# Attention, a wide first layer and a soft expert layer on one core: reordering the seam between two batches

## The chip, the cores and the metric

The kernel runs on one core of a Trainium2 chip. A core has five engines with instruction queues of their own: TensorE (PE, matrix products into PSUM), VectorE (DVE), ScalarE (ACT), GpSimd (POOL) and SyncE (SP), which here only issues the loads and stores (DMAs). Each engine takes its instructions in the order in which the program lists them and waits for other engines by semaphores. The metric is the device time of one execution in microseconds, lower is better. Before the change it is 446.04 us, the median of three runs (444.56 to 446.34).

## The reference

Three layers follow one another; all inputs are fp32 except the first layer's weights, which arrive as 64-bit floats.

1. Attention over 4 batches, 8 heads, 576 positions, 64 dimensions per head. A query sees keys in a causal window of 32 positions (heads 0 to 3), or every fourth key in a window of 128 (heads 4 to 7). `scores = q k^T / 8`, softmax over the window, times `v`.
2. `h = x @ w_in` (2304 x 512 times 512 x 2048), `g = h - tanh(h)`, `g @ w_out` (2048 x 512).
3. `logits = x @ phi` (32 slots). A softmax over all tokens gives the slots' inputs, 8 experts with two matrices and a relu work on 4 slots each, and a softmax over the slots mixes the results back for each token.

The kernel never forms the second layer's output for all tokens: it folds `phi` into `w_out` (`wp = w_out @ phi`) and takes the logits straight from `g`.

## The kernel before, in words

Heads go in pairs. `PO = (2, 3, 0, 1)` is the order of the pairs, so "the first pair" of a batch is pair 2. A pair has three units of scores, so a batch has 12 units, numbered in that order.

Batch 0's attention comes first. Its work is laid out with a small planner: `at(t, f, args)` puts a function on a list with a due time, and the list is sorted and run, so a due time only sets the place in the program order, which is the order on every engine and on SP. On the same list stand the first six row blocks of `w_out`, the first four column blocks of `w_in`, and the first two blocks of the first layer's products (`emit_h`).

A block of 64-bit weights becomes fp32 in three steps. `conv_a` (ACT, L514) takes the upper words, `conv_b` shifts them and ors in the lower words (DVE, L522 and L523). For `w_in`, `conv_in_c` then rounds to a high part (L103, on DVE for blocks 0 and 1, on ACT for 2 and 3) and subtracts it from the value, which gives the low part (POOL, L536). The products need both: `emit_h` adds `w_hi x_hi + w_hi x_lo + w_lo x_hi` (L581 to L583) over four parts of the depth. For `w_out`, `conv_out_c` and `conv_out_d` transpose the block, multiply it with `phi` (L555, copied by DVE) and store the fp32 block to DRAM (L551).

From then on chunk 0 (batch 0's first 512 tokens) goes through the first layer in eight mixed steps `s = 0 .. 7`, two blocks a step, and batch 1's attention is done inside them: `mixed_step`. The order within a step is, in short: the step's weight loads (`load_w`), batch 1's loads (`an.load`), the first block's products, `turn_qk`, the norms of the last scores, tanh (ACT, L587) and subtraction (DVE, L590) of the block, the second block likewise, the transposes of the last probabilities (PE, L408), conversions, the scores of units 2s and 2s + 1 (mask product L344, scores L366, maxima on DVE L381, exponentials on ACT L384), `scale_q` for the pair that is turned next, and the logits (L599). `QKS = (0, 1, 2, 4)` are the steps in which the four pairs are turned.

Batch 1's q and k are loaded in blocks of 32 x 32 (`load_qk_blocks`, L245 and L247, eight DMAs of 72 KB a pair in runs of 128 bytes). `scale_q` multiplies q by 1/8 on ACT (L255). `turn_qk` transposes k (L267) and then q (L268) on DVE into one of two buffers. The scores read that buffer. Batch 1's first pair is loaded during batch 0's attention.

The raw 64-bit weights of the first steps lie in `gt`, the buffer for the transposed `g`, in four places (`RAW`), so a weight load waits until the block that lay there has been shifted. Step 1's load of `w_out` (block 8) takes the place of block 6, which step 0 converts; step 2's load of block 10 takes that of `w_in` block 4.

The lines that the change touches set these places: the time of `conv_a("in", 3)`, the time of `conv_in_c` for blocks 0 and 1, the time of `scale_q(1, PO[0])`, the `turn_qk` of the first pair, and the table of `an.load(nqk, nv)`: up to how many pairs of q and k, and of v, are loaded by that step. Before, the table has `0: (3, 2)`: step 0 loads the second pair's q, k and v and the third pair's q and k.

Of the kernel before, what the change touches and what calls it, by code (L numbers as in the profile page):

```python
# [32 lines left out]
PO = (2, 3, 0, 1)  # L33
# [31 lines left out]
def moe_kernel(ctx: ExitStack, tc: tile.TileContext, q, k, v, w_in, w_out, phi, w1, w2, out):  # L65
# [186 lines left out]
    def scale_q(b, p):  # L252
        t = raws[b, p]
        if b in EA:
            nc.scalar.activation(out=t[:, 0], in_=t[:, 0], func=ACTF.Copy, scale=0.125)  # L255
        else:
            nc.gpsimd.tensor_scalar(out=t[:, 0], in0=t[:, 0], scalar1=0.125, scalar2=None, op0=ALU.mult)

    def turn_qk(b, p):

        if not qks:
            t = sb.tile([128, 2, 2 * S], F32, tag="qk", name="qk")
            qks.append(Ring([t[:, 0], t[:, 1]]))
        t = raws[b, p]
        qT[b, p] = qks[0].next()
        kT[b, p] = qT[b, p][:, S:2 * S]
        nc.vector.transpose(out=kT[b, p], in_=t[:, 1])  # L267
        nc.vector.transpose(out=qT[b, p][:, 0:S], in_=t[:, 0])  # L268
# [202 lines left out]
    def emit_lows():  # L471
        while lows:
            lows.pop(0)()
# [4 lines left out]
    def load_w(kind, ft):  # L478

        if ft % 2:  # L480
            return
        place = RAW.get((kind, ft))
        if place is None:
            t = unit("raww", [128, 1024], I64)
        else:
            t = gt[:, 4 * place:4 * place + 4].rearrange("p a b -> p (a b)").bitcast(I64)
        if kind == "in":
            t = t.rearrange("p (k f) -> p k f", k=KT)
            nc.sync.dma_start(out=t, in_=w_in[:, 128 * ft:128 * ft + 256].rearrange("(k p) f -> p k f", p=128))
            w = t.bitcast(U32).rearrange("p k (i f two) -> p two i k f", i=2, two=2)  # L490
        else:
            t = t.rearrange("p (i d) -> p i d", i=2)
            nc.sync.dma_start(out=t, in_=w_out[128 * ft:128 * ft + 256, :].rearrange("(i p) d -> p i d", p=128))
            w = t.bitcast(U32).rearrange("p i (d two) -> p two i d", two=2)
        for i in range(2):
            raw_t[kind, ft + i] = w[:, 0, i], w[:, 1, i]
# [12 lines left out]
    def conv_a(kind, ft):  # L509

        f = convs[kind].next()
        hw = raw_t[kind, ft][1].bitcast(F32)

        nc.scalar.activation(out=like(f, kind), in_=hw, func=ACTF.Prelu, scale=2.0 ** -112, alpha=-2.0 ** 32)  # L514
        cvt[kind, ft] = f

    def conv_b(kind, ft):
        wl, _ = raw_t.pop((kind, ft))
        f = cvt[kind, ft]
        du = f.bitcast(U32)  # L520
        dk = like(f, kind).bitcast(U32)
        nc.vector.tensor_scalar(out=du, in0=du, scalar1=3, scalar2=None, op0=ALU.logical_shift_left)  # L522
        nc.vector.scalar_tensor_tensor(  # L523
            out=dk, in0=wl, scalar=29, in1=dk, op0=ALU.logical_shift_right, op1=ALU.bitwise_or
        )
# [14 lines left out]
    def conv_out_c(ft):  # L540
        f = cvt["out", ft]
        ps = mm([128, 4, 128])
        for dt in range(4):
            nc.tensor.transpose(ps[:, dt, :], f[:, 128 * dt:128 * dt + 128], ident)
        wt = convs["wt"].next()
        copy(ENGS["wt"][ft % 2], wt, ps)
        wstate["wt", ft] = wt

    def conv_out_d(ft):
        f = cvt.pop(("out", ft))  # L550
        nc.sync.dma_start(out=wo_dram[128 * ft:128 * ft + 128, :], in_=f)  # L551
        wt = wstate.pop(("wt", ft))
        part = mm([128, 128])
        for dt in range(4):
            nc.tensor.matmul(  # L555
                part[32 * dt:32 * dt + 32, :], lhsT=phi_sb[:, dt, :], rhs=wt[:, dt, :],
                start=True, stop=True, tile_position=(0, 32 * dt),
            )
        if ft % 4 == 0:
            wstate["wq"] = convs["wq"]  # L560
        copy(ENGS["wq"], wstate["wq"][:, ft % 4, :], part)

    def conv_out_e(ft):
        if ft % 4 == 3:
            wq = wstate.pop("wq")
            ps = mm([128, 4, 32])
            for i in range(4):
                nc.tensor.matmul(ps[:, i, :], lhsT=wq[:, i, :], rhs=stack[:, 0, :], start=True, stop=True)
            copy(ENGS["wp"], wp[:, ft - 3:ft + 1, :], ps)
# [4 lines left out]
    def emit_h(xh, xl, ft, ps=None, part=range(KT)):  # L574

        if ps is None:
            ps = ps_h.tile([128, 512], F32, tag="h", name="h")[:, 0:xh.shape[-1]]
        for n in part:
            kt = PO[n]
            wh, wl = win(0, ft)[:, kt, :], win(1, ft)[:, kt, :]  # L580
            nc.tensor.matmul(ps, lhsT=wh, rhs=xh[:, kt, :], start=(n == 0), stop=False)  # L581
            nc.tensor.matmul(ps, lhsT=wh, rhs=xl[:, kt, :], start=False, stop=False)  # L582
            nc.tensor.matmul(ps, lhsT=wl, rhs=xh[:, kt, :], start=False, stop=(n == KT - 1))  # L583
        return ps

    def emit_tanh(ps, g):
        nc.scalar.activation(out=g, in_=ps, func=ACTF.Tanh)  # L587

    def emit_sub(ps, g):
        nc.vector.tensor_tensor(out=g, in0=ps, in1=g, op=ALU.subtract)  # L590
# [13 lines left out]
    def emit_gT(ch, ft, g):  # L604

        nc.vector.transpose(out=gt[:, ft, :], in_=g)  # L606
# [279 lines left out]
    def emit_first(ch, xh, xl, ft, first):  # L886

        return emit_h(xh, xl, ft, first[ft], range(3, KT)) if ch == 0 and ft < 2 else emit_h(xh, xl, ft)

    with tc.manual_schedule():  # L890
# [4 lines left out]
        def at(t, f, *args):  # L895
            steps.append((t, len(steps), f, args))

        for b, (t0, dt) in enumerate((ATT0,)):
            for i in range(NU):
                t = t0 + dt * i  # L900
# [18 lines left out]
        for e in range(KA):  # L919
            t, dt = WO1[0] + WO1[1] * e, WO1[1]  # L920
# [6 lines left out]
        for e in range(4):  # L927
            t, dt = WI[0] + WI[1] * e, WI[1]
            at(t - LWI if e < 2 else 45.0, load_w, "in", e)
            at(t, conv_a, "in", e)  # L930
            at(t + 3.3, conv_b, "in", e)
            at(t + (5.4 if e < 2 else 3.4), conv_in_c, e)
        first = []
        for i in range(2):

            at(ATT0[0] + ATT0[1] * (12.6 + 0.4 * i), lambda i: first.append(emit_h(xhi[0], xlo[0], i, part=range(3))), i)
        at(56.0, scale_q, 1, PO[0])
        for _, _, f, args in sorted(steps, key=lambda s: s[0:2]):
            f(*args)
        emit_lows()  # L940
# [14 lines left out]
        def mixed_step(an, ch, s, xh, xl, gs, posts):  # L955

            a, b = 2 * s, 2 * s + 1
            if s < 5:
                load_w("out", 6 + a)
            if s < 6:  # L960
                load_w("in", 4 + a)
            an.load(*{0: (3, 2), 2: (4, 3), 3: (4, 4)}.get(s, (0, 0)))
            pa, gs[a] = emit_first(ch, xh, xl, a, first), gring.next()
            if s in QKS:
                turn_qk(an.b, PO[QKS.index(s)])
            an.norms(s - 1)
            if s:
                for n in (a - 2, a - 1):
                    emit_gT(ch, n, gs[n])
            emit_tanh(pa, gs[a])  # L970
            if 0 < s < 7:
                conv_a("in", 2 + a)
                conv_a("in", 2 + b)
            emit_sub(pa, gs[a])
            emit_lows()
            if 0 < s < 7:
                conv_b("in", 2 + a)
            pb, gs[b] = emit_first(ch, xh, xl, b, first), gring.next()
            emit_tanh(pb, gs[b])
            emit_sub(pb, gs[b])  # L980
            if 0 < s < 6:
                conv_out_c(4 + a)
                conv_out_c(5 + a)
            an.trans(s)
            if s in (2, 4, 6):
                conv_out_e(3 + a)
            if 0 < s < 6:
                conv_out_d(4 + a)
                conv_out_d(5 + a)
            if 0 < s < 7:  # L990
                conv_in_c(2 + a)
                conv_b("in", 2 + b)
                conv_in_c(2 + b)
            if s < 5:
                conv_a("out", 6 + a)
                conv_a("out", 7 + a)
            an.score(2 * s, 2 * s + 1)
            if s < 5:
                conv_b("out", 6 + a)
                conv_b("out", 7 + a)  # L1000
            an.values(s)
            if s + 1 in QKS:
                scale_q(an.b, PO[QKS.index(s + 1)])
            if s:
                emit_logits(ch, a - 1, gs[a - 1])
            emit_logits(ch, a, gs[a])
# [36 lines left out]
        QKS = (0, 1, 2, 4)  # L1043
        an = Attn(1)
        an.nqk, an.nv, posts = 1, 1, None
        for ch in range(4):
# [34 lines left out]
            an, posts = nxt, last_posts  # L1081
# [198 lines left out]
```

## Time and profile before

The profiled execution took 444.48 us, its span (first to last instruction) 442.7 us, so 1.8 us lie around the span.

| | busy, us | share of the span |
|---|---|---|
| PE products | 413.1 | 93% |
| PE weight loads | 303.4 | 69% |
| DVE | 254.1 | 57% |
| ACT | 204.7 | 46% |
| POOL | 77.2 | 17% |

Shares of the chain of work that ended last over the whole span: PE 60%, issue 13%, DVE 11%, ACT 9%, DMA 3%, SP's queue 2%.

How to read it. The chain is followed back from the last instruction: at each step to what released it, or to the instruction before it on its engine. Busy shares are means over stages: in the attention of batch 0 and in the mixed steps (to about 130 us) DVE is busy five to nine tenths of a slice and ACT two to eight tenths, in the later chunks both less and PE nine tenths. The granted clock of PE is 9 tenths or more in 38 of 40 slices of the span; it is lower in the slice from 55 to 66 us and in the last one. In a timeline, a row's first number is its start, the second its duration (several instructions of one kind are merged, "x2"), and the bracket at the end gives the engine's idle time before it and what ended it. For SP, a duration is the time that the issue took, not that of the transfer.

### The profile page before, as it was taken

What the parts mean: (1) busy time and instruction counts of PE and PEld (TensorE: products, weight loads), DVE (VectorE), ACT (ScalarE), POOL (GpSimd) and SP (SyncE); (2) the same over time, 40 slices, a digit from 0 to 9 for tenths busy, and PEclk for the clock granted to TensorE, in tenths of its full rate; (3) what the DMA queues carried; (4) which work ended last, traced back from release to release, by engine and by line L of the source; (5) the groups of instructions that cost most, each with busy time, mean ns of one, the idle gap of its engine ahead of it and who ended that gap; (6) DMA issues with size and microseconds to landing.
All of it is one profiled execution on the core that took longest, in us unless ns stands there. A gap on an engine that the chain in (4) does not pass through costs nothing.

```text
span 442.7 us, 11369 instructions
## 1 busy us (share of the span) xinstructions
PE 413.1 (93%) x4564; PEld 303.4 (69%) x4564; DVE 254.1 (57%) x611; ACT 204.7 (46%) x707; POOL 77.2 (17%) x95
## 2 busy tenths in 40 slices
PE   6989979998999999999999999999999999999980
PEld 4766658876777767877767777776777688556330
DVE  1576688989976767765767865636444332223050
ACT  3677668778862546563363655231121233223040
POOL 3131233232344312122030311000000000010000
PEclk9999989999999999999999999999999999999996
DMA  8989899799567032522405203292005599999938
GB/s 228 253 206 301 237 188 278 227 285 318 178 109 130 2 51 46 95 41 66 94 5 90 44 2 97 80 415 79 0 1 179 185 408 409 364 403 407 394 134 304
DMA packets 102022, 81.17 MB, mean 183 GB/s; under 512 B 78032, under 2 KB 81872, under 8 KB 101968
## 3 DMA queue, kind: packets, MB, share of 16 engines
q1 hardware_dynamic: 101968, 80.43, 60.7%
q8 instruction: 36, 0.59, 0.6%
q14 instruction: 18, 0.15, 0.1%
HBM read 71.50 MB, written 8.91 MB: 182 GB/s over the span
## 4 chain that ended last, share of the span: by engine, by line
PE 60%; issue 13%; DVE 11%; ACT 9%; DMA 3%; SPq 2%; POOL 1%; POOLq 0%; ACTq 0%
PE h L581 10%; PE h L583 9%; PE h L582 9%; ACT mem L384 5%; PE mm L366 3%; PE h L806 3%; PE y L833 3%; PE lg L599 3%; PE mm L721 3%; PE mm L408 3%; PE mm L429 3%; PE warm L209 2%; SPq L247 2%; DMA wo_dram<-cva 1%; DVE gt L606 1%
## 5 line engine op out<-in xcount | busy, mean ns | idle before, releaser
L581 PE MATMUL h<-xhi,wts 128*128 128x512 f32 x256 | 104.9, 410 | 0.0
L583 PE MATMUL h<-xhi,wts 128*128 128x512 f32 x256 | 100.6, 393 | 0.8 <-POOL wts L536 0.8
L582 PE MATMUL h<-xlo,wts 128*128 128x512 f32 x256 | 100.5, 393 | 0.0
L587 ACT ACTIVATE mem<-h 128x512 f32<-128x512 f32 x72 | 42.8, 596 | 111.1 <-PE h L583 103.7
L590 DVE TENSOR_TENSOR mem<-h,mem 128x512 f32<-128x512 f32 x72 | 48.7, 678 | 62.6 <-ACT mem L587 62.6
L399 POOL TENSOR_TENSOR mem<-mem 128x320 f32<-128x320 f32 (+1 forms) x48 | 33.0, 695 | 159.7 <-DVE mem L398 71.4
L581 PEld LDWEIGHTS h<-xhi,wts 128*128 128x128 f32 x256 | 48.6, 190 | 15.6 <-issue 5.7
L583 PEld LDWEIGHTS h<-xhi,wts 128*128 128x128 f32 x256 | 48.4, 189 | 12.4 <-POOL wts L536 1.6
L582 PEld LDWEIGHTS h<-xlo,wts 128*128 128x128 f32 x256 | 48.6, 190 | 8.9
L606 DVE STREAM_TRANSPOSE gt<-mem 128x512 f32<-128x512 f32 x64 | 41.0, 682 | 0.0
L384 ACT ACTIVATE mem<-mem 128x80 f32<-128x80 f32 (+1 forms) x84 | 29.7, 355 | 15.9 <-DVE mem L381 15.9
L384 ACT ACTIVATE mem<-mm,mem 128x80 f32<-128x80 f32 (+1 forms) x84 | 26.6, 328 | 12.8 <-DVE mem L396 7.9
L103 ACT COPY mem<-mm 80x448 f32<-80x448 f32 (+4 forms) x64 | 25.7, 435 | 6.1 <-PE mm L408 5.0
L408 PE MATMUL mm<-mem 112*80 112x112 f32 (+1 forms) x168 | 23.8, 271 | 3.1 <-POOL mem L399 1.8
L429 PE MATMUL mm<-mem,v 80*64 80x48 f32 (+1 forms) x672 | 26.0, 226 | 0.5 <-ACT mem L103 0.5
L599 PE MATMUL lg<-mem 128*32 128x128 f32 x576 | 24.7, 280 | 1.3 <-ACT mem L621 0.7
L429 PEld LDWEIGHTS mm<-mem,v 80*64 80x64 f32 (+1 forms) x672 | 22.1, 137 | 4.6 <-ACT mem L103 1.0
L366 PE MATMUL mm<-qk 64*64 64x96 f32 (+2 forms) x672 | 23.4, 246 | 1.8 <-DVE qk L268 1.8
L366 PEld LDWEIGHTS mm<-qk 64*64 64x64 f32 (+1 forms) x672 | 17.9, 132 | 8.3 <-issue 4.6
L408 PEld LDWEIGHTS mm<-mem 112*80 112x80 f32 (+1 forms) x168 | 16.0, 122 | 8.6 <-POOL mem L399 4.1
L599 PEld LDWEIGHTS lg<-mem 128*32 128x32 f32 x576 | 13.6, 109 | 12.1 <-issue 9.0
L465 DVE TENSOR_TENSOR xlo<-mm,xhi 128x144 fp32r<-128x144 f32 (+4 forms) x72 | 15.9, 265 | 7.0 <-ACT xhi L103 7.0
(188 smaller groups left out, 632.1 us busy)
## 6 DMA issues: line engine op xcount, KB each, us to landing
ex<-in_moe_w_dram SPq DMA_DIRECT2D x21, 1024.0 KB, 11.1
gt<-in_moe_w_out_dram SPq DMA_DIRECT2D x7, 1024.0 KB, 7.4
gt<-in_moe_w_in_dram SPq DMA_DIRECT2D x7, 1024.0 KB, 8.8
gt<-in_moe_w_dram SPq DMA_DIRECT2D x6, 1024.0 KB, 10.0
mem<-in_moe_w_dram SPq DMA_DIRECT2D x5, 1024.0 KB, 7.2
wo_dram<-cva SPq DMA_DIRECT2D x16, 256.0 KB, 6.1
wo<-wo_dram SPq DMA_DIRECT2D x4, 1024.0 KB, 7.3
out_dram<-o SPq DMA_DIRECT2D x8, 512.0 KB, 4.8
```

The lines of the kernel that those rows point to most:

```text
L366: nc.tensor.matmul(ps[64 * y:64 * y + nr, c, :], lhsT=qT[b, p][r, q0:q0 + step * (nr - 1) + 1:step], rhs=kT[b, p][r, k0:k0 + step * (nk - ...
L384: nc.scalar.activation(out=pr[:, c, :], in_=ps[:, c, :], func=ACTF.Exp, bias=nm[:, c:c + 1], accum_out=sm[:, c:c + 1],)
L399: nc.gpsimd.tensor_tensor(out=pr, in0=pr, in1=rc.unsqueeze(2).to_broadcast([128, nb, nk]), op=ALU.mult)
L408: nc.tensor.transpose(ps[:, c, :], pr[0:P, c, :], ident[0:P, 0:P])
L429: nc.tensor.matmul(o[64 * hh:64 * hh + 64, col:col + nq], lhsT=vt[b, p](n, hh), rhs=pt[:, c, 64 * (x ^ sw):64 * (x ^ sw) + nq], start=True ...
L581: nc.tensor.matmul(ps, lhsT=wh, rhs=xh[:, kt, :], start=(n == 0), stop=False)
L582: nc.tensor.matmul(ps, lhsT=wh, rhs=xl[:, kt, :], start=False, stop=False)
L583: nc.tensor.matmul(ps, lhsT=wl, rhs=xh[:, kt, :], start=False, stop=(n == KT - 1))
L587: nc.scalar.activation(out=g, in_=ps, func=ACTF.Tanh)
L590: nc.vector.tensor_tensor(out=g, in0=ps, in1=g, op=ALU.subtract)
L599: nc.tensor.matmul(lgs[ch][row:row + 32, 0:128], lhsT=wp[:, ft, :], rhs=g[:, 128 * j:128 * j + 128], start=(ft < step), stop=(ft >= NFT - ...
L606: nc.vector.transpose(out=gt[:, ft, :], in_=g)
```

## The change

On the planner's list, block 3's `conv_a` moves 0.65 earlier (before the conversion of block 2 is finished by `conv_in_c`), `conv_in_c` of block 1 moves ahead of `conv_out_d` of the `w_out` blocks 4 and 5 (block 0's keeps its place in the order), `scale_q` of batch 1's first pair moves from 56.0 to 53.0, ahead of the last `emit_pv` of batch 0, and `turn_qk` of that pair comes onto the list at 54.85, behind `conv_b` of block 2 and ahead of its `conv_in_c` and of `conv_b` of block 3. In the mixed steps, step 0 no longer turns a pair, and the third pair's q and k are loaded in step 1, behind that step's two weight loads, instead of in step 0.

```diff
         for e in range(4):
             t, dt = WI[0] + WI[1] * e, WI[1]
             at(t - LWI if e < 2 else 45.0, load_w, "in", e)
-            at(t, conv_a, "in", e)
+            at(t if e < 3 else t - 0.65, conv_a, "in", e)
             at(t + 3.3, conv_b, "in", e)
-            at(t + (5.4 if e < 2 else 3.4), conv_in_c, e)
+            at(t + (5.25 if e < 2 else 3.4), conv_in_c, e)
...
-        at(56.0, scale_q, 1, PO[0])
+        at(53.0, scale_q, 1, PO[0])
+        at(54.85, turn_qk, 1, PO[0])
...
-            an.load(*{0: (3, 2), 2: (4, 3), 3: (4, 4)}.get(s, (0, 0)))
+            an.load(*{0: (2, 2), 1: (3, 2), 2: (4, 3), 3: (4, 4)}.get(s, (0, 0)))
             pa, gs[a] = emit_first(ch, xh, xl, a, first), gring.next()
-            if s in QKS:
+            if s and s in QKS:
                 turn_qk(an.b, PO[QKS.index(s)])
```

## Rows read from the trace of the kernel before

**Rows 1.** Waits of PE, 44 to 130 us: us in total, times, longest.
```profile
PE mm L366 <- DVE qk L268: 1.8, 1, 1.8
PE h L583 <- POOL wts L536: 0.6, 1, 0.6
```

**Rows 2.** Timeline of the seam, 54 to 64 us, all engines.
```profile
55.19 0.29 DVE L103 COPY cvb<-mm 128x128 f32<-128x128 f32 x1 [1.72 <-PE mm L555]
...
55.89 0.28 ACT L103 CAST xhi<-mm 128x144 fp32r<-128x144 f32 x1 [2.93 <-PE mm L429]
55.89 1.28 POOL L536 TENSOR_TENSOR wts<-mem,wts 128x512 fp32r<-128x512 f32 x1 [4.07 <-DVE wts L103]
...
56.54 0.92 DVE L522 TENSOR_SCALAR cvb<-cvb 128x512 uint32<-128x512 uint32 x1
...
59.31 0.67 ACT L255 ACTIVATE rqk<-rqk 128x576 f32<-128x576 f32 x1
...
59.44 1.06 DVE L522 TENSOR_SCALAR mem<-mem 128x512 uint32<-128x512 uint32 x1 [1.26 <-ACT mem L514]
...
60.39 0.44 PE L344 MATMUL mm<-mem 64*128 64x320 bf16 x2
60.54 0.69 DVE L523 SCALAR_TENSOR_TENSOR mem<-gt,mem 128x512 uint32<-128x512 uint32 x1
61.15 0.77 DVE L267 STREAM_TRANSPOSE qk<-rqk 128x576 f32<-128x576 f32 x1
...
62.50 1.25 DVE L590 TENSOR_TENSOR mem<-h,mem 128x512 f32<-128x512 f32 x2
...
63.37 0.48 PE L599 MATMUL lg<-mem 128*32 128x128 f32 x8
```

**Rows 3.** Timeline, DVE, shifts of step 0 with POOL idle.
```profile
64.47 0.41 DVE L522 TENSOR_SCALAR cva<-cva 128x512 uint32<-128x512 uint32 x1
...
65.97 0.69 DVE L523 SCALAR_TENSOR_TENSOR cva<-gt,cva 128x512 uint32<-128x512 uint32 x1
```

**Rows 4.** Busy time by window: us, five engines, granted clock, DMA share, GB/s.
```profile
64.00:67.00 3.00, 3.00 (x8) 2.32 (x9) 2.93 (x7) 2.80 (x18) 0.00 (x0) 0.50 1.30 208
```

**Rows 5.** Timeline of SP: weight loads of steps 0, 1, 2 and 3.
```profile
49.50 0.88 SPq L489 DMA_DIRECT2D gt<-in_moe_w_in_dram  x1
...
68.38 0.43 SPq L493 DMA_DIRECT2D gt<-in_moe_w_out_dram  x1
...
74.72 0.38 SPq L493 DMA_DIRECT2D gt<-in_moe_w_out_dram  x1
79.20 0.38 SPq L489 DMA_DIRECT2D gt<-in_moe_w_in_dram  x1
...
91.51 0.49 SPq L493 DMA_DIRECT2D raww<-in_moe_w_out_dram  x1
```

**Rows 6.** Lines L247 (50 to 64 us), L245 (79 to 90): issue ns, first and last start.
```profile
L247 SPq DMA_DIRECT2D rqk<-in_k_dram x4: 496/740/1212, 58.6 to 61.4; - x4
...
L245 SPq DMA_DIRECT2D rqk<-in_k_dram x4: 496/502/1009, 86.2 to 88.3; - x4
```

**Rows 7.** DMA issues near 61.4, 88.3 and 91.5 us: KB, median us to landing.
```profile
rqk<-in_k_dram SPq DMA_DIRECT2D x2, 72.0 KB, 2.8
...
rqk<-in_k_dram SPq DMA_DIRECT2D x2, 72.0 KB, 2.7
...
raww<-in_moe_w_out_dram SPq DMA_DIRECT2D x1, 1024.0 KB, 7.5
```

**Rows 8.** Timeline, mixed step 2 and the end of step 3's conversions.
```profile
79.03 0.77 DVE L267 STREAM_TRANSPOSE qk<-rqk 128x576 f32<-128x576 f32 x1
...
80.45 0.78 DVE L268 STREAM_TRANSPOSE qk<-rqk 128x576 f32<-128x576 f32 x1 [0.65 <-ACT rqk L255]
...
83.11 0.35 PEld L408 LDWEIGHTS mm<-mem 112*80 112x80 f32 x4 [0.42 <-POOL mem L399]
...
100.33 1.22 ACT L514 ACTIVATE cva<-raww 128x512 f32<-128x512 f32 x2
```

## The prediction, before the result was known

> **What bounds the kernel now.** I read the table of busy times first: TensorE (PE) is busy 93% of the span, so in most stages only its own work counts. Then the granted clock over the span, which is whole except near the end and in one slice, around 55 to 66 us. That is the seam between batch 0's attention and the first h step, and it is where the change lies. The table of PE's waits between 44 and 130 us [rows 1] shows what PE lost there: 1.8 us on the turned q and k of batch 1's first pair, 0.6 us on the low words of the second first-layer block. The timeline of the seam [rows 2] shows why the turn is late: VectorE (DVE) does the shifts of blocks 2 and 3 first (L522, L523) and sits idle for block 3's words from ScalarE (ACT); ACT itself sits idle 2.93 us before 55.89 and scales q only at 59.31. The scaling and the two turns (from 61.15) wait for nothing but their place in the order.
>
> From the second mixed step to about 120 us the chain of work that ended last runs mostly through DVE and ACT, not PE. In step 2 the turn of q waits 0.65 us for ACT, and PE's transposes wait 0.42 us for the probabilities that come after it [rows 8]. So a delay on DVE or ACT there reaches PE, and after that PE is so full that nothing gives it back.
>
> **Part 1: block 1's low words sooner.** conv_in_c(1) moves ahead of two copies of conv_out_d on DVE, which wait for PE anyway: DVE idles 1.72 us before 55.19 [rows 2], so it is free from 53.5. Its cast and GpSimd's (POOL's) subtraction, 1.28 us [rows 2], are done by about 55.2, when PE is still in the products before block 1. PE's 0.6 us wait goes, and PE reaches the mask product of the scores at 59.8 instead of 60.4. On the other engines nothing is added.
>
> **Part 2: scaling and turning ahead.** scale_q, 0.67 us [rows 2], falls into ACT's idle 2.93 us: free. If ACT had no such hole it would cost its 0.67 us. The block 3 words move ahead of it and of block 2's cast, so DVE no longer idles for them. DVE then runs: block 2's shift at 56.54 as before, but POOL's subtraction is no longer beside it. With POOL beside it L522 took 0.92 us [rows 2], without it 0.41 us [rows 3]. So block 2 ends at 56.54 + 0.41 + 0.69 = 57.6. The two turns now take from 61.15 to 62.50, 1.35 us up to the next start [rows 2]; behind block 2 they end at 59.0. Block 3's L522 starts there instead of at 59.44. But now POOL's subtraction of block 2 lies beside it until about 59.7, so I let it last to 60.0, and L523 starts at 60.0 instead of 60.54: a gain of 0.5 us, not more (bounds: 0.4 with the old duration of 1.06 us, 1.1 if it runs unhindered).
>
> What is late next on PE: the scores can run from 60.2, when the turned q and k are there. Behind them on PE stand the logits (L599), which need DVE's first subtraction of the step (L590), which needs ACT's tanh, which stands behind ACT's cast of block 3, which needs L523. That chain has moved only 0.5 us: 62.50 becomes 62.0, and the logits at 63.37 become 62.9 [rows 2]. So of 1.8 + 0.6 us on PE about 0.5 us reaches the next step; the rest is idle time put behind the scores instead of ahead of them. DVE's last shift of the step, which ends at 65.97 + 0.69 = 66.66 [rows 3], ends at about 66.15.
>
> The clock: the granted clock is 0.50 from 64 to 67 [rows 4], the lower level of 1.2 GHz, after PE's thin stretch from 60.4 to 63.4. In the changed order the thin stretch is from 59.8 to 62.9, about as long, so I leave this cost in, moved. If it went, 3 us at half rate would give back 1.5 us on PE.
>
> **Part 3: the third pair's loads.** This is the part that can cost. The sync queue (SP) issues in order. Today the third pair's q and k, eight loads, go out in step 0, and step 1's two 1 MB weight loads follow from 68.38 [rows 5]. After the change the weights stand first. The first of them must wait for the shift that ends at 66.15 (its place in gt holds the words that are shifted), so the two go out at about 66.15 and 66.6, two microseconds sooner than now, and the eight small loads behind them. Then come step 1's two stores and step 2's loads.
>
> How long do q and k take behind such weights? The trace has two cases. In step 0 the second weight load went out at 49.50, with the first half a microsecond ahead, and the last k at 61.4, landing 2.8 us later, at 64.2: 14.7 us [rows 5 to 7]. In step 2 the weight load went out at 79.20, the other one 4.5 us ahead of it, and the last k at 88.3, landing at 91.0: 11.8 us [rows 5 to 7]. From 66.6 that is 78.4 to 81.3. The new place is like step 0's in its order, but with less in flight before it, so I take the middle, 79.85.
>
> When is k needed? L267 of step 2 starts at 79.03 now [rows 8]; with the gain of 0.5 it would be 78.5. L268 follows at 80.45 since it waits for ACT; that would be 79.95. With k at 79.85, L267 runs 0.77 us from then and L268 starts at about 80.65: 0.2 us later than before. The gain is gone. At the low end (78.4) it stays; at the high end L268 is at 82.1, 1.65 us late. Behind L267 on DVE queue the reciprocals that POOL's products and PE's transposes wait for, so this passes to PE in full.
>
> By the Trainium skill, "DMA: Bandwidth & Descriptors", section "Anatomy of one DMA", a transfer takes about 2.0 us and its bytes at 436 GB/s (stated for the software path). For these 2.7 MB an estimate by that page is 8.2 us, k landing near 74.3, well in time. The trace does not agree: a single weight load of 1 MB took 7.5 us to land [rows 7]. The same page's section "Queues, rings and completion order" says that each engine takes descriptors in ring order, which speaks against putting the small loads behind the large ones.
>
> The second place is step 3. The weight load for out-block 12 went out at 91.51 and landed 7.5 us later, at 99.0; ACT takes it at 100.33 [rows 5, 7, 8], so it has 1.3 us to spare. After the change out-block 10's load no longer goes out at 74.72 but behind the eight small loads and the two stores, near 79. Step 2's loads then find the queue as step 0's did. From the weight load to the first k it took 58.6 - 49.5 = 9.1 us in step 0 and 86.2 - 79.2 = 7.0 us in step 2 [rows 5, 6]; so what follows goes out up to 2.1 us later, out-block 12's words land up to 101.1, and ACT is up to 0.8 us late there. Below nothing this cannot go, since the order only puts more ahead of it.
>
> **Sum.** The two late points are not added: a delay at the first moves the need at the second too. Between 0.2 us (the turn) and 0.8 us (the words) I take +0.5 us. In the profiled execution 444.48 us (span 442.7 and 1.8 around it) becomes 445.0. That execution lay 1.56 us under the median of the three timed runs, which spread from 444.56 to 446.34; I put the same +0.5 on the median: 446.5 us. A change under 0.5%, 2.2 us, cannot be told from none here, so "same" reaches from 443.8 to 448.3.
>
> **Rivals.**
> - Loads in time. k lands by 78.4, out-block 12 by 100: the 0.5 us of the seam stays, up to 1.1 us if block 3's shift runs unhindered. 445.5, down to 444.9. For it: less is in flight at 66 than at 49. This is also where the page's law for transfers would put it. Against: both rows of the trace put k at or past the need.
> - Loads too late, the slower side. k at 81.3 or later: L268 is 1.65 us late, step 2's stores and loads go out 1.4 us later still, and out-block 12's words come 0.8 + 1.4 = 2.2 us late. 447.7 to 448.3; if SP is held longer than in step 0, 449. It decides once k lands after 79.6, and passes the limit of 0.5% only with both places at their worst. For it: step 0's case, the one with the same order.
> - PE decides alone. If the steps after the seam follow PE and not DVE and ACT, the 1.8 + 0.6 us of [rows 1] come in full: 443.6; with the clock up as well, 442.1. Against: the logits' wait for L590. The Trainium skill, "TensorE: Matmul & The Clock Gate", section "HAM oscillation", has idle gaps between products as what lowers the clock; the trace agrees as far as [rows 4] follow such a gap, but the gap does not go here, it moves.
> - The change does not do what it says: if the scaling waits in ACT's order for something else, the turn stays late and nothing moves, 446.0.
>
> **Chances.** Forecast 0.40 (its own range 445.8 to 447.0), loads in time 0.25, too late 0.19, PE alone 0.10, no effect 0.06. Faster by over 0.5%: nearly all of PE alone and a little of loads in time, 0.13. Slower: the worst half of too late and a remainder for what I don't see, 0.14. Same: 0.73. The range leaves out PE alone below and the tail of too late above: 444.3 to 448.4.
>
> **What would show it.** Right: in the changed profile no wait of PE for L268 at the seam, the two turns near 57.6, an idle PE between scores and logits of about 1.8 us, a half clock still near 63 to 67, the first weight load of step 1 near 66, and DVE waiting for a k load before L267 of step 2, or ACT for a weight load before out-block 12. Wrong: no idle PE after the scores (then PE decides), k landed before 78, or the loads of step 2 going out as early as now. A clock at full through the first h step would make it faster than I say.

## The result, and the profile after

The changed kernel takes 448.94 us, the median of four runs (448.43 to 453.58), beside 445.30 for the kernel before on the same chip (443.96 to 446.34): a ratio of 1.0112, 95% interval 1.0072 to 1.0153. It is slower by 1.1%. The prediction was wrong: 446.5 was forecast, 448.4 was the upper end of the range, and "slower" had a chance of 0.14. The profiled execution took 448.43 us, its span 446.6, against 444.48 and 442.7.

The seam does what the change says. Waits of PE, 44 to 130 us, in the changed kernel (us in total, times, longest; against [rows 1]):

```profile
PE mm L408 <- POOL mem L399: 3.8, 4, 2.4
PE lg L599 <- DVE mem L590: 2.1, 1, 2.1
```

Timeline of its seam (against [rows 2]):

```profile
55.91 0.42 DVE L522 TENSOR_SCALAR cvb<-cvb 128x512 uint32<-128x512 uint32 x1
...
56.97 0.77 DVE L267 STREAM_TRANSPOSE qk<-rqk 128x576 f32<-128x576 f32 x1
...
58.32 1.04 DVE L522 TENSOR_SCALAR mem<-mem 128x512 uint32<-128x512 uint32 x1
...
58.78 0.44 PE L344 MATMUL mm<-mem 64*128 64x320 bf16 x2
...
59.40 0.69 DVE L523 SCALAR_TENSOR_TENSOR mem<-gt,mem 128x512 uint32<-128x512 uint32 x1
...
62.01 0.42 PE L599 MATMUL lg<-mem 128*32 128x128 f32 x8 [2.05 <-DVE mem L590]
```

Both waits of [rows 1] are gone, and one of 2.05 us stands behind the scores instead, ahead of the logits. The logits start at 62.01, not 63.37. This execution was already 0.64 us ahead at 52 us, in a part that the change does not touch, so the seam gave 0.72 us. The wait of 2.4 us at L408 is new. Where it comes from shows in the order of SP (start, length of the issue; against [rows 5, 6]):

```profile
65.54 0.38 SPq L493 DMA_DIRECT2D gt<-in_moe_w_out_dram  x1
65.98 0.46 SPq L489 DMA_DIRECT2D gt<-in_moe_w_in_dram  x1
66.55 6.09 SPq L245 DMA_DIRECT2D rqk<-in_q_dram  x4
72.69 4.11 SPq L245 DMA_DIRECT2D rqk<-in_k_dram  x4
76.85 0.97 SPq L551 DMA_DIRECT2D wo_dram<-cva  x2
77.93 0.40 SPq L493 DMA_DIRECT2D gt<-in_moe_w_out_dram  x1
78.43 0.43 SPq L489 DMA_DIRECT2D gt<-in_moe_w_in_dram  x1
78.96 9.20 SPq L245 DMA_DIRECT2D rqk<-in_q_dram  x4
...
93.30 0.49 SPq L493 DMA_DIRECT2D raww<-in_moe_w_out_dram  x1
```

The third pair's eight small loads hold SP from 66.55 to 76.80. Out-block 10's words go out at 77.93 instead of 74.72, and the fourth pair's q behind them takes 9.20 us to go out, where it took 6.44. Out-block 12's words go out at 93.30, 1.79 us later than before, while the engines stand earlier. Before the change SP had idle time in this stretch. Its two stores of step 1 were out by 70.91:

```profile
69.58 1.33 SPq L551 DMA_DIRECT2D wo_dram<-cva  x2
```

It then stood idle for 3.8 us ahead of the load at 74.72 and for 4.1 us ahead of the one at 79.20 [rows 5], each time until DVE's shift (L523) had freed the place in `gt`. The moved loads use this idle time up: in the changed kernel SP goes from one issue to the next, and from 78.5 us on the chain of work that ended last runs through its issues up to out-block 12's load. What waits for the two late loads, in the timelines of DVE, ACT and PE in the changed kernel (against [rows 8]):

```profile
79.27 0.78 DVE L267 STREAM_TRANSPOSE qk<-rqk 128x576 f32<-128x576 f32 x1 [1.47 <-DMA rqk<-in_k_dram]
79.98 0.73 DVE L268 STREAM_TRANSPOSE qk<-rqk 128x576 f32<-128x576 f32 x1
...
101.16 1.24 ACT L514 ACTIVATE cva<-raww 128x512 f32<-128x512 f32 x2 [1.33 <-DMA raww<-in_moe_w_out_dram]
...
107.55 0.53 PE L408 MATMUL mm<-mem 128*96 128x128 f32 x3 [2.38 <-POOL mem L399]
```

ACT waits 1.33 us for the words, everything behind it on ACT is late by that, and in step 4 PE waits 2.38 us for the probabilities. In the kernel before it waited 0.90 us there:

```profile
106.70 0.53 PE L408 MATMUL mm<-mem 128*96 128x128 f32 x3 [0.90 <-POOL mem L399]
```

Then the granted clock falls. PE's busy time by window in the changed kernel (us, PE busy, granted clock, DMA share, GB/s); the kernel before has 1.00 in every one of these windows:

```profile
106.00:108.00 2.00, 0.45 (x3) 1.00 0.95 344
108.00:110.00 2.00, 1.57 (x16) 1.00 1.03 410
110.00:112.00 2.00, 2.00 (x38) 0.59 1.02 345
112.00:114.00 2.00, 2.00 (x40) 0.50 0.76 286
114.00:116.00 2.00, 2.00 (x19) 0.50 0.68 155
116.00:118.00 2.00, 2.00 (x8) 0.71 1.03 399
```

PE is full from 110 to 118 and runs at 1.2 GHz for most of it. The same instruction in both traces gives the account, after minus before, in us:

| event | after - before | step |
|---|---|---|
| before the seam, 52 us | -0.64 | nothing of the change |
| logits of step 0 | -1.36 | seam, -0.72 |
| mask product of step 2 | -0.81 | third pair's k, late: +0.5 |
| logits of step 3 | -0.64 | +0.2 |
| L514 on out-block 12, and PE's L408 behind it | +0.83, +0.85 | words late: +1.5 |
| logits of step 5 | +3.1 | half clock: +2.2 |
| first expert product (L833), 412.6 us | +3.1 | nothing comes back |
| end of the span | +3.9 | a late expert load: +0.8 |

The last step is hardly the change's: by the DMA issues from 340 us on, the 16 expert loads into `ex` landed 12.2 us after their issue in this execution and 11.1 in the one of before, and PE waited 0.6 us for a later one, into `gt`. Of the 13 other profiles of this study, two more have loads that slow (11.9 and 12.1 us, in kernels that do not differ there), with waits of 0.6 and 2.0 us; in the rest they land within 11.4 us.

### The profile page after: what moved, and what is told of

The parts are those of the page before. It is cut to its first block, busy times and chain, and to the rows that moved or that the text cites. A ratio compares the mean times of both kernels' runs of the same rounds, so it can differ in the third digit from the quotient of the medians.

```text
span 446.6 us, 11368 instructions
## 1 busy us (share of the span) xinstructions
PE 415.4 (93%) x4564; PEld 305.2 (68%) x4564; DVE 251.6 (56%) x611; ACT 205.5 (46%) x707; POOL 77.5 (17%) x95
## 4 chain that ended last, share of the span: by engine, by line
PE 58%; issue 12%; ACT 8%; DMA 8%; DVE 6%; SPq 3%; POOL 1%; POOLq 0%; ACTq 0%; DVEq 0%
PE h L581 10%; PE h L583 9%; PE h L582 9%; DMA gt<-in_moe_w_dram 4%; ACT mem L384 4%; PE lg L599 3%; PE mm L366 3%; PE mm L408 3%; PE mm L721 3%; PE mm L429 3%; PE h L806 3%; SPq L245 3%; DMA rqk<-in_q_dram 2%; PE warm L209 2%; DMA raww<-in_moe_w_out_dram 2%
## 5 line engine op out<-in xcount | busy, mean ns | idle before, releaser
L590 DVE TENSOR_TENSOR mem<-h,mem 128x512 f32<-128x512 f32 x72 | 48.9, 680 | 66.9 <-ACT mem L587 66.8
L408 PE MATMUL mm<-mem 112*80 112x112 f32 (+1 forms) x168 | 23.7, 271 | 5.1 <-POOL mem L399 3.8
L599 PE MATMUL lg<-mem 128*32 128x128 f32 x576 | 25.1, 283 | 3.3 <-DVE mem L590 2.7
L599 PEld LDWEIGHTS lg<-mem 128*32 128x32 f32 x576 | 13.9, 110 | 14.3 <-issue 9.0
L408 PEld LDWEIGHTS mm<-mem 112*80 112x80 f32 (+1 forms) x168 | 16.0, 122 | 10.6 <-POOL mem L399 6.2
## 6 DMA issues: line engine op xcount, KB each, us to landing
ex<-in_moe_w_dram SPq DMA_DIRECT2D x21, 1024.0 KB, 12.1
gt<-in_moe_w_dram SPq DMA_DIRECT2D x6, 1024.0 KB, 11.4
```

The costliest lines, as they stand in the source:

```text
L408: nc.tensor.transpose(ps[:, c, :], pr[0:P, c, :], ident[0:P, 0:P])
L599: nc.tensor.matmul(lgs[ch][row:row + 32, 0:128], lhsT=wp[:, ft, :], rhs=g[:, 128 * j:128 * j + 128], start=(ft < step), stop=(ft >= NFT - ...
```

## The experiments

Each kernel was timed against the kernel before on the same chip, in groups on four chips, where that took 443.9 to 444.3 us; the changed kernel's own row is from the comparison above. In each, one half of the change is undone or one delay is made by itself. A run's mean clock is the granted clock averaged over its span, with 1 for 2.4 GHz. By an estimate from the windows of these traces, the half clock of step 4 takes about .01 off it (7 to 10 us of 444 at half rate), so .985 parts most runs that had such a loss from those that had none; where a run had it, the mean does not say. The kernel before is not free of it: beside these kernels it has .985 or more in 86 of 109 runs. The results of the main ones together:

| kernel | median, us (runs) | ratio to before, 95% interval | runs with a mean clock of .985 or more |
|---|---|---|---|
| changed | 448.94 (4) | 1.0112, 1.0072 to 1.0153 | 0 |
| seam part alone | 443.28 (12) | 0.9987, 0.9963 to 1.0010 | 10 |
| loads part alone | 448.71 (6) | 1.0090, 1.0055 to 1.0126 | 1 |
| before, late words alone | 449.67 (12) | 1.0100, 1.0071 to 1.0128 | 2 |
| seam part, ACT late alone | 447.83 (11) | 1.0075, 1.0046 to 1.0104 | 1 |
| the same, PE's wait filled | 444.61 (12) | 1.0015, 1.0000 to 1.0030 | 10 |
| changed, wait half filled | 447.40 (12) | 1.0052, 1.0023 to 1.0082 | 4 |
| changed, wait filled | 444.81 (12) | 1.0002, 0.9981 to 1.0023 | 12 |
| changed, out 12 earlier | 445.96 (12) | 1.0019, 0.9985 to 1.0054 | 5 |

**Which half costs.** The seam part alone is the changed kernel with the old table of loads:

```diff
-            an.load(*{0: (2, 2), 1: (3, 2), 2: (4, 3), 3: (4, 4)}.get(s, (0, 0)))
+            an.load(*{0: (3, 2), 2: (4, 3), 3: (4, 4)}.get(s, (0, 0)))
```

> The seam edits alone, with the load table of the kernel before. Theory T (the third pair's loads make out-block 12's words late in step 3; ACT waits 1.3 us for them, PE then waits over 2 us, and its clock falls to half for some 6 us): about 0.7 us under the kernel before (445.3), so 444.6; no ACT wait for a weight load, PE's longest wait in step 4 at most 1 us, the clock whole from 105 to 120. Rival S (the moved scaling and turns cost the time): 448.9, as the changed kernel, 447 at least. Rival C (the half clock near 110 has nothing to do with the late words): no ACT wait, but the half clock stays, about 446.8.

443.28 us. ACT waits for no load, the wait at L408 is 1.4 us at the longest and 0.91 us in step 4, the clock is whole also at the seam. The loads part alone is that edit the other way round, in the kernel before:

> The kernel before with the load table of the changed one alone. T: as slow as the changed kernel or slower by the seam's 0.7 us, 448.9 to 449.6: PE's 1.8 us wait for the turn stays, ACT waits 1 to 2 us for out-block 12's words, PE over 2 us in step 4, half clock behind it. S: 445.3, as before. C: the words late, but no half clock at 110: about 446.8.

448.71 us, the whole loss. Its profile has the same chain in the same place: waits of ACT and PE (first fence: timeline; second: busy time by window).

```profile
101.57 1.22 ACT L514 ACTIVATE cva<-raww 128x512 f32<-128x512 f32 x2 [1.73 <-DMA raww<-in_moe_w_out_dram]
...
107.95 0.53 PE L408 MATMUL mm<-mem 128*96 128x128 f32 x3 [2.56 <-POOL mem L399]
```

```profile
108.00:110.00 2.00, 1.56 (x10) 0.88 0.99 398
110.00:112.00 2.00, 2.00 (x22) 0.50 1.00 304
112.00:114.00 2.00, 2.00 (x34) 0.50 0.96 356
114.00:116.00 2.00, 2.00 (x40) 0.50 0.35 89
```

So the seam is not where the time went, and the third pair's loads are.

**Late words by themselves.** In the kernel before, step 3's two weight loads change places; nothing else moves, the third pair's loads least of all.

```diff
-            if s < 5:
+            if s < 5 and s != 3:
                 load_w("out", 6 + a)
             if s < 6:
                 load_w("in", 4 + a)
+            if s == 3:
+                load_w("out", 6 + a)
```

> The kernel before with step 3's two weight loads in the other order: out-block 12's words go out behind in-block 10's, nothing else changes. T: the words land 1 to 3 us after their time, ACT waits for them, PE's wait in step 4 grows past 2 us and the half clock comes: 447.0 to 449.0. S: 445.3. C: the words late but no half clock: 446.3 to 446.8.

449.67 us. The profiled execution was one of the two short ones, and it tells the two costs apart:

```profile
101.01 1.23 ACT L514 ACTIVATE cva<-raww 128x512 f32<-128x512 f32 x2 [1.17 <-DMA raww<-in_moe_w_out_dram]
```

ACT waits 1.17 us, PE's wait at L408 is 2.1 us, the clock is 1.00 from 102 to 122 us all the same, and the execution takes 445.32, 1.3 us above the 444.06 of the kernel before on that chip. The ten runs with a mean clock of .983 or less take 447.7 to 451.1. No profile shows how late the words were in those ten: in the thirteen profiles of this study that issue this load in step 3 it landed 7.1 to 10.0 us after its issue, so the delay itself can vary.

**A late ACT without a late load.** In the seam part alone, where no load is late, ACT does its conversions of out-blocks 12 and 13 twice over.

```diff
-        nc.scalar.activation(out=like(f, kind), in_=hw, ...)
+        for _ in range(2 if (kind, ft) in (("out", 12), ("out", 13)) else 1):
+            nc.scalar.activation(out=like(f, kind), in_=hw, ...)
```

> The kernel with the seam part alone (old load table: no load is late), in which ACT does its two conversions L514 of out-block 12 twice over in step 3: 2 x 0.62 = 1.24 us more work on ACT in the place where the changed kernel waited 1.33 us for the words. Theory T (ACT's lateness is the whole of it; how it comes about does not matter): PE waits 2 us or more on POOL at L408 in step 4, the half clock comes behind it in most runs, and the median is 447 us or more against 443.3 for the kernel without the doubled work. Rival (the queues' traffic of the stretch is what costs, or the clock falls by other means): the time rises by no more than the 1.2 us of added work, to 444.5.

447.83 us, 4.55 above the kernel without the doubled work (3.9 by the ratios to before, as the two ran on different chips), for 1.42 us more on ACT (2.64 against 1.22). Timeline, and busy time by window:

```profile
98.20 2.64 ACT L515 ACTIVATE cva<-raww 128x512 f32<-128x512 f32 x4
...
105.98 0.53 PE L408 MATMUL mm<-mem 128*96 128x128 f32 x3 [2.29 <-POOL mem L399]
```

```profile
106.00:108.00 2.00, 1.56 (x12) 0.97 1.01 333
108.00:110.00 2.00, 2.00 (x22) 0.50 0.94 350
...
116.00:118.00 2.00, 2.00 (x7) 0.50 0.89 345
118.00:120.00 2.00, 2.00 (x10) 0.97 0.04 13
```

No load is late here, and the loss is the same. What counts is that ACT is late there. The added work is the same in every execution of this kernel; one run of eleven has a mean clock of .986, at 444.37 us, the others have .981 or less, at 446.3 to 451.0 us.

**The same delay, without PE's wait.** Into that kernel go 30 idle products, whose result is not read, ahead of step 4's transposes.

```diff
+    def fill(n):
+        ps = mm([128, 256])
+        w = ident.bitcast(BF16)
+        for _ in range(2 * n):
+            nc.tensor.matmul(ps, lhsT=w[:, 0:128], rhs=w, start=True, stop=True)
...
+            if s == 4:
+                fill(15)
             an.trans(s)
```

> The kernel in which ACT is late by doubled work (447.83 us), with the 30 idle products in PE's queue ahead of step 4's first transposes: by 3.44 us for 30 they run from about 103.5 to 107, where PE waited 2.3 us on POOL before. ACT is late here in every execution, so the words' own varying lateness plays no part. Theory T (the half clock behind PE's wait is the larger part of the loss): the clock stays whole in 106 to 118, nearly every run has a mean clock of .985 or more, and the median falls to that of the seam part alone plus the delay itself, 1.2 to 1.6 us: 444.5 to 445.2. Rival (the delay itself costs more than its length, by what it pushes at the end): the clock is whole and the median stays at 447 us or more. Third: the clock is halved all the same, 447 us or more.

444.61 us, within the 444.5 to 445.2 expected. Timeline, and busy time by window (its lines lie six further down than in that kernel):

```profile
98.75 2.63 ACT L521 ACTIVATE cva<-raww 128x512 f32<-128x512 f32 x4
...
104.04 3.44 PE L216 MATMUL mm<-mem 128*128 128x256 bf16 x30
107.53 0.99 PE L414 MATMUL mm<-mem 128*96 128x128 f32 x6
```

```profile
108.00:110.00 2.00, 2.00 (x30) 1.00 0.64 245
...
116.00:118.00 2.00, 2.00 (x11) 1.00 0.98 382
```

ACT is as late as in the kernel above, PE has no wait, and the clock stays whole. Between the two kernels nothing but the fill differs, so the half clock is 447.83 - 444.61 = 3.2 us (2.7 by the ratios, 0.6% of 444), and the delay itself 444.61 - 443.28 = 1.3 us (1.2 by the ratios). Two of the twelve runs still have a mean clock of .978, at 445.5 and 445.9 us; where they lost it no profile shows.

**Filling the wait in the changed kernel.** First 18 products, `fill(9)`, then 30, `fill(15)`, in the same place.

> The changed kernel with 18 idle bf16 products (1.9 us at the full clock) on PE in step 4, ahead of the transposes that PE waits for. T: ACT's wait for the words stays, PE's idle time there shrinks by 1.9 us, the clock stays whole from 108 to 118, and some 2.2 us come back: 446.7. If the half clock has another cause (C) it stays: 448.9; and if the transposes weren't what PE waited for, the products cost their 1.9 us: 450.8.

447.40 us. In its profile ACT waits 1.24 us for the words, the 18 products take 2.13 us, and PE still waits 1.25 us behind them; the clock is 0.50 from 110 to 114, and once more from 430 us to the last products at 437. Four of twelve runs have a mean clock of .985 or more, and they take 443.95 to 446.1 us. The expectation was half met: the median fell, and with part of the wait left the clock held in some runs only.

> The changed kernel with 30 idle products (128x256, bf16, result not read) in PE's queue ahead of step 4's first transposes, where 18 were before: by the 2.13 us that 18 took they run 3.55 us, from 104.1 to 107.6, over the whole of the wait. Theory T with the clock as the larger part: PE has no wait over 0.5 us there, the granted clock stays whole through 108 to 118 in most runs, and the median is 1.3 to 1.5 us above the kernel before's (the lateness alone), about 445.5 us. Rival (the loss is the late words' own and what they push, not the clock): the clock is whole and the median is still 447.5 us or more. A third outcome, the clock halved though PE was never idle, would say that a wait of PE is not what brings it.

444.81 us, and no run of twelve under a mean clock of .985. In the profiled execution the words happened to be in time (they went out at 91.21 us and landed 7.2 us later, and ACT waited for no load), so this profile does not show a late ACT beside a whole clock; the kernel with ACT late by doubled work does. Up to the fill the program is that of the changed kernel, whose four runs all have a mean clock of .979 or less.

**The load moved instead.** Out-block 12's words are asked for in step 2, ahead of the fourth pair's loads.

```diff
-            if s < 5:
+            if s < 5 and s != 3:
                 load_w("out", 6 + a)
             if s < 6:
                 load_w("in", 4 + a)
+            if s == 2:
+                load_w("out", 12)
```

> The changed kernel with one thing moved: out-block 12's words are asked for at the end of the mixed step 2's weight loads, ahead of the fourth pair's loads, instead of at the head of step 3. Theory T (the words of out-block 12 are what costs, with the half clock that comes behind the wait they cause): L514 of step 3 waits for no load, PE's wait on POOL at L408 in step 4 falls from 2.4 us to about 0.9, the clock of 110 to 116 us is whole, and the time is that of the kernel with the seam part alone, 443.3 us, within 1 us. Rival R (the stretch has more to carry than its queues give, and whichever load comes last there is late): the fourth pair's q and k or in-block 10 take over the wait, ACT or DVE waits 1 us or more on them, and the time stays at 447 us or above.

The place is mended as theory T has it: L514 starts at 98.61 without a wait, the clock is 1.00 from 104 to 122 us, and the first expert product starts at 407.8 us, where the seam part alone has it too. But the median is 445.96, 2.7 us above that kernel and not within 1 us of it (1.4 us by the ratios, whose intervals overlap). In the profiled execution the loss lies at the end:

```profile
PE y L833 <- DMA gt<-in_moe_w_dram: 2.0, 1, 2.0
```

The expert loads landed 12.1 us after their issue here, and behind PE's wait of 2.0 us the granted clock is 0.50 from 424 to 426: the same pair of costs, in another place. Six of the other runs have mean clocks of .981 or less; no profile shows where, so for these the cause is open.

**Attempts to get more from the seam.** The seam part alone, with 16 idle products in PE's wait ahead of the logits of step 0:

```diff
+            else:
+                fill(8)
             emit_logits(ch, a, gs[a])
```

> The kernel with the seam part alone, with 16 idle products (128x256, bf16, result not read) in PE's queue ahead of the mixed step 0's logits L599, where PE waits 2.05 us on DVE's L590: about 1.9 us of work in a wait of 2.05. If the clock falls at the seam in many runs of the kernel with the seam part alone (its runs lie from 442.6 to 447.4 with mean clocks of .991 to .978), the fill keeps it and the median falls by up to 1 us, to about 442.5. If the runs' spread has another place, nothing changes (443.3 within 0.7).

445.39 us, ratio 1.0006 (0.9976 to 1.0035). Five runs of twelve lie at 442.2 to 445.0 with clocks of .990 or more, the others at 445.2 to 448.0. The profile is one of these. Waits of ACT, and PE's busy time by window:

```profile
ACT cva L520 <- DMA gt<-in_moe_w_out_dram: 1.5, 1, 1.5
```

```profile
60.00:64.00 4.00, 3.79 (x30) 1.00 0.76 121
...
80.00:84.00 4.00, 1.62 (x9) 0.73 1.08 359
84.00:88.00 4.00, 4.00 (x48) 0.50 0.47 77
88.00:92.00 4.00, 4.00 (x72) 0.50 0.90 176
```

The clock at the seam is whole, as wanted. In step 1 the words of out-block 8 are 1.45 us late, PE waits up to 2.9 us a step later, and some 12 us of half clock follow: the same chain, one load sooner. The seam part alone can have the late words too. Its second measurement:

> The kernel with the seam part alone once more, beside the two above on one chip: 443.3 us, 0.1 to 0.3% under the kernel before, as in its first measurement.

443.88 us, ratio 0.9987 (0.9965 to 1.0009), as in the first. In the profile of this one ACT waited 1.36 us in step 1 for out-block 8, and the clock there held. At the seam it did not, though PE waits as long there as in the first profile, 2.0 us at L599. PE's busy time by window in the first profile (clock 1.00) and in this one (0.66):

```profile
60.00:64.00 4.00, 2.76 (x18) 1.00 1.01 201
```

```profile
60.00:64.00 4.00, 2.51 (x13) 0.66 0.51 83
```

Out-block 8's words asked for in step 0 were to cure that:

> The kernel with the seam part alone, with out-block 8's words asked for in the mixed step 0, ahead of the third pair's q and k, instead of at the head of step 1. If their lateness in step 1 (ACT waited 1.45 us for them in the kernel with the seam fill) is what spreads the runs of the seam part alone, the runs over 444 us go and the median falls by up to 0.5 us, to about 443. Rival: the third pair's k, now behind another load, comes late in step 1, DVE waits on it, PE waits over 1 us in step 2, and the median is 445 us or more.

> The kernel of the seam fill with the same load of out-block 8's words in step 0. Theory: the fill keeps the clock whole at the seam, which brings PE into step 1 sooner; the words, asked for sooner too, are no longer late there; nearly all runs lie where the good ones of the seam fill lay, at 442.2 to 443.3 us, median 442.8. Rival: as for the kernel before this one, the third pair's k is late instead, 445 us or more.

443.78 us (ratio 0.9986, 0.9960 to 1.0012) and 446.17 us (1.0038, 1.0015 to 1.0062). Neither tests the idea. Block 8 lies in the place of block 6, so in these two kernels blocks 6 and 7 are made from block 8's words, and ACT waits for the load in step 0 instead (1.99 us in the first). Step 4 is as in the seam part alone, and there the profile of the first shows something else: PE waits no longer than in the kernel before, and the clock falls all the same.

```profile
106.97 0.53 PE L408 MATMUL mm<-mem 128*96 128x128 f32 x3 [0.91 <-POOL mem L399]
```

```profile
110.00:112.00 2.00, 2.00 (x34) 0.50 0.95 313
```

So a longer wait is not needed for the half clock; it made it the usual case, by the table above. The best kernel of the study stays the seam part alone: 1.2% faster than the changed kernel, and not measurably faster than the kernel before.

## Why the prediction was wrong

- **Right: the seam.** The turns came at 56.97 and 57.66 (forecast: ended at 59.0, they ended at 58.4), the logits' wait for L590 took the gain's place, and 0.72 us were left of 2.4 (forecast 0.5). PE alone did not decide.
- **Right: the third pair's k.** With this execution's lead of 0.64 us, the forecast of 79.85 is 79.2; L267 got its k at 79.27. The gain was gone in step 2, as forecast: L268 0.17 us later than before once the lead is taken off, forecast 0.2.
- **Right in place, short in size: the words of out-block 12.** They were to go out up to 2.1 us later than 91.51 and land at 101.1 at the latest. They went out at 93.30, took 7.8 us and landed at 101.1, the upper bound. ACT was late by 1.33 us, not 0.8, since it came to L514 at 99.83 instead of 100.33. The push on SP was also larger than the 2.1 us that I took for the most: from in-block 10's load to out-block 12's it took 14.87 us, against 12.31 before, 2.56 more; the load of in-block 10 had gone out 0.77 us sooner, which hides part of it. The cost on PE was 1.5 us.
- **Wrong, the step that failed: the Sum.** It takes "+0.5 us" from two late points and ends there. Behind the second point stood a wait of PE, and I never asked what that wait does next. I looked at the granted clock in the one place where [rows 4] show it low, the seam, and left it in, "moved"; a new wait of 2.4 us in step 4 got no price. Without the half clock the seam's gain and the two late points come to 1.5 us in the table above (-0.7 + 0.5 + 0.2 + 1.5), three times the +0.5 and still inside the range. The half clock cost 2.2 us in this trace and 2.7 to 3.2 us by the two kernels that differ in the fill alone, about twice the delay that brought it. With [rows 4] at hand I could have put 1.5 us and more on it, as I did for the clock at the seam.
- **The rival "Loads too late"** had the side right, at 447.7 to 448.3, but by another sum: 0.8 + 1.4 us from a k at 81.3. k was in its middle place; the words alone did it, and its upper end has no half clock either.
- **The Trainium skill**, "TensorE: Matmul & The Clock Gate", section "HAM oscillation", which I cited for the seam, describes the same order of events as in step 4: products, a wait for a transfer, products at the lower level. The waits of its example are longer than those here. The traces agree with the order, by 0.50 behind waits of 2.29 to 2.56 us, and by the kernel with doubled work the wait need not be for a transfer. In the page's example the loss comes every time; here it came or not behind the same wait (2.0 us at L599 in the two profiles of the seam part alone), and the measurement decides.

What stays open: why the clock holds behind 2.1 us of waiting in one execution of late words and falls behind 0.91 us in another kernel, and where the runs with out-block 12 loaded earlier lose theirs.

## What to carry to other kernels

A delay that ends as idle time of a full PE is to be priced twice: its length, and the half clock that can follow it at full load (here 1.3 and about 3 us), the second with a chance, as it doesn't come every time. When loads on one in-order queue are moved, list the queue's idle time and each later load's slack against its use: eight small loads behind two weight loads cost the third weight load after them 1.79 us, and it had 1.3. And time the halves of such a change apart: the seam half alone lost nothing, the loads half cost 4 to 4.7 us.

## What the runs showed of the hardware

- The same wait gives two outcomes. In two profiles of the seam part alone PE waits 2.0 us at L599, and from 60 to 64 us the clock is 1.00 in one and 0.66 in the other. In step 4 it fell to 0.50 behind waits of 2.29 to 2.56 us, and also behind 1.25 us (wait half filled) and 0.91 us (out-block 8 asked for in step 0); it held behind 2.15 us (late words alone).
- How much of the wait is filled changes how often the clock holds: with 18 products, and 1.25 us of waiting behind them in the profile, 4 runs of 12 have a mean clock of .985 or more, with 30 products all 12.
- The issue of a small load has no fixed price: loads of 72 KB took 0.5 to 1.2 us of issue each in [rows 6], but four of them held SP for 6.09 us at 66.55 and for 9.20 us at 78.96, each time behind two weight loads just issued. Before the change the second of these took 6.44 us, with the two weight loads 4.5 us apart [rows 5], and four at 63.53, 14 us behind the last weight load, took 2.17 us.
